# Columns of the norm gain in a PSUM bank of their own, and the second group's input issued by GpSimd: a start-up edit in a one-core convolution and MLP kernel

## The chip, the cores and the metric

The kernel runs on one core of a Trainium2 chip. The metric is the device time of one execution in microseconds (us). A profiled execution also has a span, from its first to its last instruction; times inside a profile are counted from the start of that span.

## What is computed

The reference has two blocks, one after the other. x is (8, 4224, 192) in float32, with 8 heads of 24 channels and 7 taps a head; the second block has a hidden width of 768. The weights of the second block arrive as float64.

```python
# block 1: lightweight convolution, causal, 7 taps per head
w = exp(weight - max(weight)); w = w / (sum(w) + 1e-9)       # (8 heads, 7 taps)
out[b, s, h, :] = sum_k w[h, k] * x_padded[b, s + k, h, :]    # 6 zero rows in front

# block 2: norm, two matrix products, residual
xn = (x - mean(x)) / sqrt(var(x) + 1e-6) * g_ln
result = x + relu(xn @ w_ch1) @ w_ch2
```

## The kernel before

**Groups.** The sequence positions lie on the 128 partitions. The work is cut into 18 groups of at most 16 positions a partition (`groups`, L70). Group 0 has 6 positions of batch 0. Group 1 has the 128 positions left over at the end of each of the 8 batches, 16 partitions a batch and 8 positions a partition. Group 2 has 10 positions, and all later ones 16. The loop at L963 takes one group at a time: up projection, the next group's convolution and transposition, down projection, result. It loads x of group g + 2 (L966), so x of groups 0 and 1 are loaded in the start-up.

**Start-up.** All instructions are issued in program order on each engine; there is no planner. What waits for what follows from the tiles that they share. The part that the edit touches is this:

- ScalarE's DMA queue loads the taps' raw weights (L197) and g in two pieces (L199, L200) into one row on one partition.
- TensorE spreads the raw weights over the 128 partitions by a product with a row of ones (L203), and turns g from a row into two columns, one a half (L205). Both write the same PSUM bank, `spread`.
- VectorE and ScalarE compute the softmax of the taps there (L268 to L277). ScalarE copies g's columns to `gs` (L273).
- SP's DMA queue loads w_ch1 (L211, L215), x of group 0 (`load_x(0)`: L164 twice, for partitions 16 to 127 and 1 to 15, and L171 for partition 0), x of group 1 (`load_x(1)`: L139 eight times, one DMA a batch of 16 partitions), and w_ch2 (L221), in this order.
- GpSimd writes the constants: averages (`share`, L296 and L297), a matrix `copy` (L299, L302), `less` (L306), `unit` (L312, L313), and the tap matrices of the last head (L319), which need the taps. ScalarE writes those of the two heads before (L327).
- float64 is turned into float32 by VectorE and ScalarE in `split_words` (L233 to L242) and `join_words` (L247 to L259). For w_ch1 `join_words` multiplies by g (L258), so it needs `gs`.

**After that, in TensorE's order.** `keep_warm(20)` (L939, L376) multiplies constants into a bank that nobody reads. `centre_w1` (L340) takes the mean out of w_ch1: L343, a convolution of one head of group 0 by matmuls (`conv_on_pe`, L334), L346, a second head, then three sets of four banks (L358, L363), with the third head behind the first set. ScalarE copies each bank of these sets to `w1` (L368). The first up projection (`up(0)`, L538) follows. The other five heads of group 0 are convolved by VectorE (L422), starting from a first tap on ScalarE (L397).

**PSUM.** There are 8 banks, handed out in a ring. `take_bank` gives the next one; `take_set` rounds up to the next bank whose number is a multiple of four and gives four:

```python
def take_set():
    i = (turn[0] + 3) // 4 * 4 % 8
    turn[0] = i + 4
    return all_banks[:, i : i + 4]
```

A matmul into a bank waits until the last reader of that bank is done. `up(0)` writes its set in the order q = 0 to 3, one bank a q.

Of the kernel before, what the change touches and what calls it, by code (L numbers as in the profile page):

```python
# [16 lines left out]
def kernel(  # L17
# [29 lines left out]
    nc = tc.nc  # L47
    PSUM = bass.MemoryType.PSUM
    B, S, D = x.shape
    H, K = weight.shape  # L50
    F = moe_w_ch1.shape[1]
    P = 128
# [66 lines left out]
    def take_bank():  # L119
        i = turn[0] % 8  # L120
        turn[0] = i + 1
        return all_banks[:, i]
# [9 lines left out]
    def load_x(g, queue=nc.sync):  # L132
        b, j0, n = groups[g]
        t = xpool.tile([P, J + PAD, D], F32, tag="xg", name=f"xg{g}")
        xg[g] = t
        flat = t.rearrange("p j d -> p (j d)")
        if b is None:
            for b in range(B):
                queue.dma_start(  # L139
                    out=flat[LP * b : LP * b + LP, 0 : (PAD + n) * D],  # L140
                    in_=bass.AP(
                        tensor=x.tensor, offset=(b * S + P * R - PAD) * D,
                        ap=[[n * D, LP], [1, (PAD + n) * D]],
                    ),
                )
            return
        if j0:
            queue.dma_start(
                out=flat[:, 0 : (n + PAD) * D], in_=xr[b, :, (j0 - PAD) * D : (j0 + n) * D]
            )  # L150
            return
        if b:

            queue.dma_start(
                out=flat[:, 0 : (PAD + n) * D],
                in_=bass.AP(
                    tensor=x.tensor, offset=(b * S - PAD) * D, ap=[[R * D, P], [1, (PAD + n) * D]]
                ),
            )
            nc.gpsimd.memset(t[0:1, 0:PAD, :], 0.0)  # L160
            return
        nc.gpsimd.memset(t[0:1, 0:PAD, :], 0.0)
        for p0, p1 in ((16, P), (1, 16)):
            nc.sync.dma_start(  # L164
                out=flat[p0:p1, 0 : (PAD + n) * D],
                in_=bass.AP(
                    tensor=x.tensor, offset=(b * S + p0 * R - PAD) * D,
                    ap=[[R * D, p1 - p0], [1, (PAD + n) * D]],
                ),
            )  # L170
        nc.sync.dma_start(out=flat[0:1, PAD * D : (PAD + n) * D], in_=xr[b, 0:1, 0 : n * D])  # L171
# [5 lines left out]
    gs = consts.tile([P, 2], F32, name="gs")  # L177
# [5 lines left out]
    def carve(n, dtype):  # L183
        part = room[:, taken[0] : taken[0] + n].bitcast(dtype)
        taken[0] += n
        return part
# [8 lines left out]
    row, ones = carve(H * K + 2 * P, F32)[0:1], carve(P, F32)[0:1]  # L195
    g_row = row[:, H * K :]
# [4 lines left out]
    nc.vector.memset(ones, 1.0)  # L201
    spread = take_bank()
    nc.tensor.matmul(spread[:, 0 : H * K], ones, row[:, 0 : H * K], start=True, stop=True)  # L203
    for r in range(2):
        nc.tensor.matmul(  # L205
            spread[:, H * K + r : H * K + r + 1], g_row[:, P * r : P * r + P], ones[:, 0:1],
            start=True, stop=True,
        )
    raw_taps = spread[:, 0 : H * K].rearrange("p (h k) -> p h k", k=K)

    nc.sync.dma_start(  # L211
# [5 lines left out]
            in_=w1_words[P:D, 2 * FH * r : 2 * FH * (r + 1)],  # L217
        )
    load_x(0)
    load_x(1)  # L220
    nc.sync.dma_start(  # L221
        out=raw2.rearrange("p (c d) w -> p c (d w)", d=D),
        in_=w2_words.rearrange("(c p) d -> p c d", p=P),
# [7 lines left out]
    def split_words(raw, mant, power):  # L231
        hi = raw[:, :, 1]
        nc.vector.tensor_single_scalar(mant.bitcast(U32), hi, 0xFFFFF, op=ALU.bitwise_and)  # L233
        nc.scalar.activation(mant.bitcast(F32), mant, AF.Relu, scale=2.0**-20, bias=1.0)
        nc.vector.tensor_scalar(
            out=power.bitcast(U32), in0=hi, scalar1=20, scalar2=0x7FF,
            op0=ALU.logical_shift_right, op1=ALU.bitwise_and,
        )
        nc.vector.tensor_scalar(
            out=power, in0=power, scalar1=896.0, scalar2=1151.0, op0=ALU.max, op1=ALU.min  # L240
        )
        nc.scalar.activation(power, power, AF.Relu, scale=float(1 << 23), bias=low)  # L242

    def join_words(dst, raw, mant, power, g=None):
        lo, hi = raw[:, :, 0], raw[:, :, 1]
        mant, power = mant.bitcast(F32), power.bitcast(U32)
        nc.vector.scalar_tensor_tensor(  # L247
            out=mant, in0=lo, scalar=2.0**-52, in1=mant, op0=ALU.mult, op1=ALU.add
        )
        nc.vector.scalar_tensor_tensor(  # L250
            out=power, in0=hi, scalar=0x80000000, in1=power,
            op0=ALU.bitwise_and, op1=ALU.bitwise_or,
        )
        power = power.bitcast(F32)
        if g is None:
            nc.vector.tensor_tensor(dst, mant, power, op=ALU.mult)
            return
        nc.vector.scalar_tensor_tensor(  # L258
            out=dst, in0=mant, scalar=g, in1=power, op0=ALU.mult, op1=ALU.mult  # L259
        )  # L260
# [9 lines left out]
        taps, raw_taps, wmax.unsqueeze(2).to_broadcast([P, H, K]), op=ALU.subtract  # L270
    )
    nc.scalar.activation(taps, taps, AF.Exp)
    nc.scalar.copy(gs, spread[:, H * K : H * K + 2])  # L273
    nc.vector.tensor_reduce(wsum, taps, axis=AX.X, op=ALU.add)
    nc.vector.tensor_scalar(wsum, wsum, scalar1=1e-9, scalar2=None, op0=ALU.add)
    nc.vector.reciprocal(wsum, wsum)
# [23 lines left out]
    for q in range(NQ):  # L300
# [19 lines left out]
        out=diag[:, H - 1 - PE_HEADS[0]], in_=taps[:, H - 1, :].unsqueeze(2).to_broadcast([P, K, P]),  # L320
        pattern=[[0, K], [-1, P]], compare_op=ALU.is_equal, fill=0.0, base=0, channel_multiplier=1,
    )

    def tap_matrices(ks):
        for k in ks:
            for i, h in enumerate(PE_HEADS[:-1]):
                nc.scalar.mul(diag[:, i, k, :], unit, taps[:, h, k : k + 1])  # L327
# [44 lines left out]
    def keep_warm(times):  # L372

        idle = take_bank()
        for _ in range(times):
            nc.tensor.matmul(idle[:, 0:P], less, copy, start=True, stop=True)  # L376

    tap_matrices(range(3))
    split_words(*words_a)
    tap_matrices(range(3, K))  # L380
    join_words(w1f[:, 0:2].rearrange("p s f -> p (s f)"), *words_a, ga)
    split_words(*words_b)
# [5 lines left out]
    def first_tap(g, heads=(0, H)):  # L388
        n = groups[g][2]
        if g == 1:  # L390

            y[g] = y[0][:, groups[0][2] :]
        elif heads[0] == 0:
            y[g] = ypool.tile([P, J, D], F32, tag="y", name=f"y{g}")
        for h in range(*heads):
            cs = slice(h * GRP, h * GRP + GRP)
            nc.scalar.mul(y[g][:, 0:n, cs], xg[g][:, 0:n, cs], taps[:, h, 0:1])  # L397
# [538 lines left out]
                add_and_store(g, js, D - C)  # L936


    keep_warm(20)  # L939
    first_tap(0, heads=(0, PE_HEADS[0]))  # L940

    early = CH * C // GRP
# [98 lines left out]
```

## Time and profile before

| what | value |
|---|---|
| median of 4 runs | 965.15 us (964.58 to 965.78) |
| profiled execution, its own time | 965.93 us |
| its span | 964.1 us |
| TensorE busy | 951.9 us, 99% of the span |
| VectorE busy | 897.9 us, 93% |
| ScalarE busy | 681.0 us, 71% |
| GpSimd busy | 250.3 us, 26% |
| SP's DMA queue (hardware_dynamic) | 6512 packets, 63.31 MB |
| GpSimd's DMA queue (software_dynamic) | 19120 packets, 99.36 MB |

Engines are called PE (TensorE's matmuls), PEld (its weight loads), DVE (VectorE), ACT (ScalarE), POOL (GpSimd) and SP. A q behind a name is the queue that issues for that engine. A float32 matmul has two passes, and each is an instruction of its own. Busy time is a sum over the whole span; what a step is worth is read from the stage in which it stands.

### The profile page before, as it was taken

To read this page: it belongs to the slowest core of one execution; us is meant where nothing else is said; L and a number is where in the kernel's file an instruction comes from. 1 tells how busy PE (TensorE), PEld (TensorE's weight loads), DVE (VectorE), ACT (ScalarE), POOL (GpSimd) and SP (SyncE) were. 2 spreads that over 40 slices of the span, in tenths; PEclk is the share of its full clock that TensorE was granted. 3 is DMA by queue.
4 is the path that set the end of the run, shared out by engine and by line. 5 is a ranking of instruction groups with operands and counts; after the bars stand their busy time and mean duration, and the time that the engine had idled before them with its cause. 6 is when DMAs were issued, how large, how long until landed. Compare 5 with 4: busy or idle time off the path is not lost.

```text
span 964.1 us, 38399 instructions
## 1 busy us (share of the span) xinstructions
PE 951.9 (99%) x17280; PEld 717.8 (74%) x17280; DVE 897.9 (93%) x1506; ACT 681.0 (71%) x1098; POOL 250.3 (26%) x383
## 2 busy tenths in 40 slices
PE   7999999999999999999999999999999999999997
PEld 6886586776858677686968778695867868586787
DVE  6999998989999999999999999999989999999867
ACT  5724669587787959687795968779696877867361
POOL 2004411612116131432116131341215221161300
PEclk9999999999999999999999999999999999999999
DMA  9343787769788796969788796978779697767031
GB/s 176 121 124 133 155 214 179 196 123 281 143 240 162 202 203 121 278 134 256 143 231 166 168 246 123 276 139 239 156 176 234 117 281 138 176 136 127 3 68 68
DMA packets 25802, 165.12 MB, mean 171 GB/s; under 512 B 3109, under 2 KB 4006, under 8 KB 17831
## 3 DMA queue, kind: packets, MB, share of 16 engines
q0 software_dynamic: 19120, 99.36, 53.5%
q1 hardware_dynamic: 6512, 63.31, 18.1%
q8 instruction: 135, 2.21, 0.9%
q14 instruction: 29, 0.24, 0.1%
q10 hardware_dynamic: 6, 0.00, 0.0%
HBM read 38.93 MB, written 50.33 MB: 93 GB/s over the span
## 4 chain that ended last, share of the span: by engine, by line
PE 94%; DMA 2%; DVE 2%; POOL 1%; issue 0%; ACT 0%; SPq 0%; DVEq 0%; POOLq 0%; ACTq 0%
PE ps L538 46%; PE ps L812 41%; PE ps L759 6%; DMA xg<-in_x_dram 1%; DVE room L779 1%; DMA room<-room 1%; PE ps L334 1%; DVE room L640 0%; ACT room L634 0%; PE ps L358 0%; PE ps L363 0%; POOL room L601 0%; POOL d L465 0%; DVE y L904 0%; POOL r L488 0%
## 5 line engine op out<-in xcount | busy, mean ns | idle before, releaser
L422 DVE SCALAR_TENSOR_TENSOR y<-xg,taps,y 128x384 f32<-128x384 f32 (+3 forms) x734 | 367.3, 577 | 0.2
L812 PE MATMUL ps<-room,w2sums 128*32 128x256 f32 (+1 forms) x4320 | 235.9, 375 | 0.2
L538 PE MATMUL ps<-yt,w 32*128 32x256 f32 (+2 forms) x4104 | 235.8, 379 | 0.1
L634 ACT COPY room<-ps 128x1024 f32<-128x1024 f32 (+1 forms) x132 | 172.0, 1303 | 79.1 <-PE ps L538 78.4
L538 PEld LDWEIGHTS ps<-yt,w 32*128 32x128 f32 x4104 | 204.8, 185 | 26.3 <-issue 9.6
L812 PEld LDWEIGHTS ps<-room,w2sums 128*32 128x32 f32 x4320 | 137.7, 110 | 93.2 <-ACT room L647 5.6
L812 PE MATMUL ps<-room,w 128*32 128x256 f32 (+1 forms) x3240 | 180.4, 375 | 0.1
L779 DVE TENSOR_TENSOR room<-room 128x1024 f32<-128x1024 f32 (+1 forms) x135 | 151.0, 1192 | 6.4 <-PE ps L812 6.4
L812 PEld LDWEIGHTS ps<-room,w 128*32 128x32 f32 x3240 | 104.0, 110 | 68.9 <-DVE room L640 5.2
L538 PE MATMUL ps<-ysums,w1sums 32*128 32x256 f32 x2160 | 125.1, 379 | 0.1
L538 PEld LDWEIGHTS ps<-ysums,w1sums 32*128 32x128 f32 x2160 | 108.8, 185 | 11.3 <-ACT room L634 3.6
L647 ACT ACTIVATE room<-room 128x1024 f32<-128x1024 f32 (+1 forms) x74 | 90.7, 1249 | 11.3 <-DMA room<-parts_cs 10.9
L818 ACT COPY cs<-ps 128x256 f32<-128x256 f32 (+1 forms) x180 | 66.6, 371 | 44.2 <-PE ps L812 44.2
L890 ACT ACTIVATE ot<-ot,r 128x192 f32<-128x192 f32 x232 | 93.8, 463 | 0.0
L897 POOL DMA_DIRECT2D out_dram<-ot x40 | 34.3, 1086 | 202.3 <-ACT ot L890 125.9
L397 ACT ACTIVATE y<-xg,taps 128x384 f32<-128x384 f32 (+3 forms) x141 | 72.7, 610 | 7.1 <-DMA out_dram<-y 6.9
L640 DVE TENSOR_TENSOR room<-room,ps 128x2048 f32<-128x2048 f32 (+1 forms) x20 | 42.5, 2127 | 35.9 <-PE ps L538 35.7
L453 DVE BATCH_NORM_STATS2 st<-y 128x6 f32<-128x192 f32 x264 | 70.2, 344 | 0.0
L538 PE MATMUL ps<-yt,w1sums 32*128 32x256 f32 x1080 | 65.3, 380 | 0.1
L818 ACT COPY room<-ps 128x256 f32<-128x256 f32 (+1 forms) x90 | 33.7, 374 | 43.8 <-PE ps L812 34.1
L538 PE MATMUL ps<-ysums,w 32*128 32x256 f32 x1080 | 64.5, 376 | 0.0
L408 ACT ACTIVATE tb<-xg,taps 128x384 f32<-128x384 f32 x112 | 62.0, 637 | 0.0
(109 smaller groups left out, 884.7 us busy)
## 6 DMA issues: line engine op xcount, KB each, us to landing
xg<-in_x_dram SPq DMA_DIRECT2D x15, 2112.0 KB, 17.7
out_dram<-ot POOLq DMA_DIRECT2D x29, 768.0 KB, 9.3
y<-tb POOLq DMA_DIRECT2D x28, 768.0 KB, 10.5
room<-room POOLq DMA_DIRECT2D x42, 512.0 KB, 5.3
out_dram<-y SPq DMA_DIRECT2D x13, 1536.0 KB, 9.6
room<-parts_cs POOLq DMA_DIRECT2D x14, 1024.0 KB, 8.2
room<-parts_tb POOLq DMA_DIRECT2D x14, 1024.0 KB, 7.6
xg<-in_x_dram SPq DMA_DIRECT2D x1, 1536.0 KB
```

Of the source, the lines that this page charges most:

```text
L397: nc.scalar.mul(y[g][:, 0:n, cs], xg[g][:, 0:n, cs], taps[:, h, 0:1])
L408: nc.scalar.mul(tb[g][:, 0:n, cs], xg[g][:, 1 : 1 + n, cs], taps[:, h, 1:2])
L422: nc.vector.scalar_tensor_tensor(out=y[g][:, 0:n, cs], in0=t[:, k : k + n, cs], scalar=taps[:, h, k : k + 1], in1=y[g][:, 0:n, cs], op0=AL ...
L453: nc.vector.bn_stats(out=sums[g][:, j, :], in_=y[g][:, j, :])
L538: nc.tensor.matmul(banks[:, q, i * w : i * w + w], right[rows, c, P * i : P * i + P], left[rows, :, c, :], start=(first and c == 0 and i = ...
L634: nc.scalar.activation(dst, src, AF.Relu) if relu else nc.scalar.copy(dst, src)
L647: nc.scalar.activation(c, c, AF.Relu)
L759: nc.tensor.matmul(bank[C * q : C * q + C, 0:w], w2[:, f, C * c : C * c + C], left, start=(f == 0), stop=(f == NF - 1),)
L779: nc.vector.tensor_tensor(a[:, *dst, f], a[:, *left, f], a[:, *right, f], op=op)
L812: nc.tensor.matmul(dst[C * q : C * q + C, 0:w], right[:, f, C * c : C * c + C], left[:, f, q], start=(first and f == PAIR), stop=(f == PAI ...
L818: nc.scalar.copy(to[:, c], dst[:, 0:w].rearrange("p (j t) -> p j t", t=t))
L890: nc.scalar.mul(ots[g][:, j, :], ots[g][:, j, :], rstd[g][:, j : j + 1])
```

## The change

Three things are edited, all in the start-up. g's columns are taken out of `spread` and get a bank of their own, `g_cols`; the 20 idle matmuls that stood in front of the first tap now stand before `tap_matrices`, 12 ahead of the two column matmuls and 8 behind them, with a bank each. The copy to `gs` moves behind the first `split_words` on ScalarE. `load_x(1)` is taken from SP's queue, where it stood between x of group 0 and w_ch2, and is issued by GpSimd behind L319, the last of its constants.

```diff
@@ -201,11 +201,6 @@
     nc.tensor.matmul(spread[:, 0 : H * K], ones, row[:, 0 : H * K], start=True, stop=True)
-    for r in range(2):
-        nc.tensor.matmul(
-            spread[:, H * K + r : H * K + r + 1], g_row[:, P * r : P * r + P], ones[:, 0:1],
-            start=True, stop=True,
-        )
     raw_taps = spread[:, 0 : H * K].rearrange("p (h k) -> p h k", k=K)
@@ -217,7 +212,6 @@
     load_x(0)
-    load_x(1)
     nc.sync.dma_start(
@@ -270,7 +264,6 @@
     nc.scalar.activation(taps, taps, AF.Exp)
-    nc.scalar.copy(gs, spread[:, H * K : H * K + 2])
     nc.vector.tensor_reduce(wsum, taps, axis=AX.X, op=ALU.add)
@@ -321,6 +314,8 @@
+    load_x(1, nc.gpsimd)
+
     def tap_matrices(ks):
@@ -375,8 +370,16 @@
             nc.tensor.matmul(idle[:, 0:P], less, copy, start=True, stop=True)
+    keep_warm(12)
+    g_cols = take_bank()
+    for r in range(2):
+        nc.tensor.matmul(
+            g_cols[:, r : r + 1], g_row[:, P * r : P * r + P], ones[:, 0:1], start=True, stop=True
+        )
+    keep_warm(8)
     tap_matrices(range(3))
     split_words(*words_a)
+    nc.scalar.copy(gs, g_cols[:, 0:2])
     tap_matrices(range(3, K))
@@ -936,7 +939,6 @@
-    keep_warm(20)
     first_tap(0, heads=(0, PE_HEADS[0]))
```

## The prediction, made before the run

> **What bounds the kernel now.** I read the page's chain of work first. TensorE carries 94% of it, DMA 2%.
>
> ```profile
> span 964.1 us, 38399 instructions
> ...
> PE 94%; DMA 2%; DVE 2%; POOL 1%; issue 0%; ACT 0%; SPq 0%; DVEq 0%; POOLq 0%; ACTq 0%
> ```
>
> So the end is set by when TensorE starts real work and by the holes after that. The edit touches only the first 30 us. Next view: the chain in order of time there (start, length, what).
>
> ```profile
> 2.48 0.58 SPq L164
> 3.06 0.05 issue
> 3.11 13.84 DMA xg<-in_x_dram
> 16.95 0.14 issue
> 17.08 1.95 PE ps L334 x14
> ...
> 27.60 0.65 PE ps L363 x8
> 28.25 13.15 PE ps L538 x288
> ```
>
> Nothing but the arrival of x of group 0 (16.95) decides when L334 starts. From 17.08 on TensorE is back to back. The third view, the timeline, has the work before the arrival and the first hole after it (start, length, engine, line; in brackets the idle time before).
>
> ```profile
> 4.62 0.21 POOL L306 MEMSET room<- 128x128 f32 x1
> ...
> 5.05 0.29 POOL L313 TENSOR_SCALAR_AFFINE_SELECT room<-room 128x128 f32<-128x128 f32 x1
> ...
> 7.84 7.38 PE L376 MATMUL ps<-room 128*128 128x128 f32 x40
> 7.94 0.22 DVE L268 TENSOR_REDUCE wmax<-ps 128x8 f32<-128x56 f32 x1 [6.88 <-PE ps L205]
> ...
> 9.70 1.24 POOL L319 TENSOR_SCALAR_AFFINE_SELECT room<-taps 128x896 f32<-128x896 f32 x1 [4.35 <-DVE taps L277]
> ...
> 15.30 1.56 PE L343 MATMUL ps<-room 128*128 128x384 f32 x4
> ...
> 26.97 3.16 ACT L368 COPY w<-ps 128x384 f32<-128x384 f32 x8 [1.20 <-PE ps L363]
> ```
>
> The softmax of the taps (L268 to L277) waits for g's columns; GpSimd (L319) and ScalarE (L327) wait for the taps. All of it is done before x lands. Fourth view, the DMA issues (count, KB each, us to landing):
>
> ```profile
> xg<-in_x_dram SPq DMA_DIRECT2D x8, 168.0 KB, 10.7
> raw<-in_moe_w_ch_dram SPq DMA_DIRECT2D x1, 1152.0 KB, 9.9
> xg<-in_x_dram SPq DMA_DIRECT2D x1, 1008.0 KB, 13.0
> ...
> xg<-in_x_dram SPq DMA_DIRECT2D x1, 135.0 KB, 13.8
> ```
>
> x of group 0 is 1008 + 135 + 4.5 KB. Behind it, in the same SP queue, stand the eight 168 KB pieces of group 1's x, then w2. I linked the trace's packet records into engines by end and next start. Each engine writes its w1 rows, then 7 or 8 rows of 9216 B of group 0, then one 10752 B row of each piece of group 1. Most engines start group 0's rows between 5.5 and 7.6 us and are done between 10.6 and 12.7. One starts at 8.42, ends its last row at 15.27, and its completion is the 16.95. A row takes about 0.57 us until 10.7, when the first group-1 rows begin; then 1.4 to 1.7.
>
> [...] from 163.5 to 169 us, engines holding both GpSimd's queue (1536 B, 0.14 us) and SP's (12288 B, 0.47 us) mostly alternate one for one. [...] group 1's pieces, each on 16 partitions, take 1.05 to 1.15 us a row on all engines, 16 x 10752 B / 1.1 us = 156 GB/s with two pieces overlapping, against some 255 GB/s for group 0's rows. [...] L235 took 1.34 us beside L319, 0.36 us for half the size later. [...] The trace shows only the warming: L376 matmuls start 0.213 us apart until 13.41 and 0.111 us after, 5.57 us from 7.84.
>
> **Part 1, g's columns apart.** L268 can follow L203 (ends 2.78), so at about 2.85 instead of 7.94. From L268 to L319 it is 9.70 - 7.94 = 1.76 us: taps at 4.6. GpSimd is busy until 5.34, so L319 runs 5.4 to 6.6. w1 lands at 7.15 (semaphore records), so L233 moves from 9.55 to about 7.2. Idle matmuls start at 4.87 (behind L306); 24 passes at 0.213 plus a slow first end near 10.2, the two columns near 11. The copy of gs, now behind split_words on ScalarE, then waits until about 11.2 (split_words ends by 9.7); queued behind it is half of tap_matrices (8 x 0.305 = 2.4 us, ends 13.7), and L258 waits for gs too. It ends near 12.4 instead of 15.24. The second idle batch runs out at 13.0 (warm) to 14.6 (cold). L343 ends near 14.6 instead of 16.86. What hides all this is the wait for x: worth 0 unless x lands before 16.95, and then at most 17.08 - 14.9 = 2.2 us.
>
> **Part 2, one bank more.** Two more take_bank calls per start (g's own, a second idle batch) shift the ring by two. Counting calls: before, the last eight L368 copies free banks 3,4,5,6 then 7,0,1,2, and the first set of up(0) is 4 to 7; its fourth matmul waits for the fifth copy (28.46 + 0.52 = 28.98; that matmul starts at 29.04). After, they free 5,6,7,0 then 1,2,3,4, and the set is 0 to 3; its fourth matmul waits for the seventh copy (29.20 + 0.55 = 29.75). In order, all of up(0) stands behind it: **+0.77 us** on the path. Later sets shift by four throughout and cost 0.
>
> **Part 3, x of group 1 on GpSimd.** SP's own issues get shorter: w2 follows group 0's x at once and lands early, wanted only at 28.66. Gain 0. Group 1's x is wanted at 32.85 (L397), so its own lateness costs 0. GpSimd has no other work until 77 us. But the eight issues, queued behind L319, now start at 6.6. Issues at 103 to 107 us come 0.5 us apart; the one at 96.94 has its first packet at 98.58, 1.64 us later. So group-1 rows enter the engines at about **8.3 us instead of 10.7**, in their own queue, and alternate with group 0's rows instead of following them. The late engine at that moment still has all 8 rows of group 0. Its floor without group 1: 8.42 + 8 x 0.5 + 1.7 to completion = 14.1. With strict alternation it writes 8 x 0.57 + 7 x 1.12 = 12.4 us: 20.8, landing 22.5. By bytes: some 664 KB of group 0 at 260 and 7/8 of 1376 KB at 156 GB/s are 2.55 + 7.7 = 10.3 us: 18.7, landing 20.4. [...] If rows of group 1 cost it only 0.66 (half the engines at them), 8.6 us: landing 18.7. I take 20.2: **+3.3 us**; bounds -2.2 and +5.5.
>
> **Sum.** +3.3 + 0.77 = +4.1 us on the profiled execution: 965.93 (span 964.1 and 1.8 around it) gives 970.0. The four runs' median is 0.8 lower, 965.15: **969.2 us**.
>
> **Rivals.** (1) *The clock falls too.* TensorE is idle from about 14.6 to 20.2, 5.6 us. [...] the matmuls after the arrival start at half speed; at 5.57 us until warm, as at the start, that loses 2.4 more: 971.6. [...] Against: no restart in the trace, [...] and a later L343 shortens the gap. (2) *x is not delayed*: [...] the late engine is spared; landing within 1 us of 16.95, bank shift alone: 965.9. For it: the same bytes move. Against: the alternation at 164 us. (3) *Not slower, faster*: [...] (1.4 to 1.7 us a row became 0.57 again) and lands at 14.5; part 1 then pays 2.2 - 0.77 = 1.4: 963.7. It decides if group-1 rows enter after about 12 us; my reading of the issue times has them at 8.3. This would also be the case in which spreading the idle matmuls does what it says.
>
> **Numbers.** Forecast, x late with a warm clock: 0.45, own range 967.1 to 970.6. (1) 0.26, to 973.5. (2) 0.20, 964.7 to 967.1. (3) 0.09, 962.5 to 964.7. A change within 0.2% (1.93 us: 963.2 to 967.1) can't be told from none. Slower is the forecast and (1), 0.70 with an edge of (2) off and on; same is (2) and most of (3), 0.25; faster the deep end of (3), 0.05. The range 965.0 to 972.6 leaves out (3) and the ends, under 0.2.
>
> **What would show it.** In the profile after: L268 near 2.9 and L319 near 5.4; GpSimd's queue with 10752 B packets from 8 to 9 us; the chain's DMA piece ending near 20 instead of 16.95; L343 ending near 14.6; the first full row of L538 about 1.6 us behind the last L363 instead of 0.8; the interval of L334 matmuls 0.122 us (warm) or double. I am wrong if group-1 packets start after 11 us or if x lands before 17.

## The result, and the profile after

The changed kernel takes **967.77 us** (median of 44 runs, 965.07 to 971.04); the kernel before takes 965.34 us beside it (62 runs, 964.02 to 969.02). The ratio is 1.0023, 95% interval 1.0019 to 1.0028: slower by 2.4 us, just above the 0.2% that can be told from no change. The profiled execution took 967.13 us, with a span of 965.3, 1.2 over that of before. The forecast number was 969.2, and it was off by 1.4 us. Its mechanism was wrong: x of group 0 landed earlier (12.51, from the semaphore records, instead of 16.95), not later, and the loss arose some 15 us further on.

The page's span and chain of work. DMA's share has doubled, from 2% to 4%:

```profile
span 965.3 us, 38415 instructions
...
PE 93%; DMA 4%; DVE 1%; POOL 1%; ACT 0%; issue 0%; ACTq 0%; POOLq 0%; DVEq 0%
```

The chain in order of time (start, length, what) shows which DMA it is. Before, x of group 0 held it until 16.95; now it is w2 (`raw`), until 28.73, and then the split of w2 on VectorE and ScalarE, up to an eviction (L531):

```profile
0.80 4.95 DMA room<-in_moe_w_ch_dram
...
5.76 22.97 DMA raw<-in_moe_w_ch_dram
...
28.76 0.76 DVE spare L227
29.52 0.68 DVE spare L229
...
32.18 0.80 ACT room L531
...
33.02 9.76 PE ps L541 x192
42.79 11.84 PE ps L762 x288
```

The timeline of TensorE has the front of it (start, length; in brackets the idle time before). The first products of `centre_w1` (L338, L343 before) follow at once on the idle matmuls (L371; the 24 instructions of its line are `keep_warm(12)`, two a matmul), and the first convolution (L329, L334 before) on L338: it starts at 13.84 instead of 17.08 and waits for no DMA. Then `up(0)` breaks after 96 instructions:

```profile
4.88 5.33 PE L371 MATMUL ps<-room 128*128 128x128 f32 x24 [2.04 <-POOL room L299]
...
12.55 1.46 PE L338 MATMUL ps<-room 128*128 128x384 f32 x4
13.84 1.88 PE L329 MATMUL ps<-xg,room 128*128 128x144 f32 x14
...
25.38 5.31 PE L541 MATMUL ps<-yt,w 32*128 32x192 f32 x96 [0.41 <-ACT w L363]
33.02 9.76 PE L541 MATMUL ps<-yt,w 32*128 32x192 f32 x192 [2.34 <-ACT room L531]
```

In the kernel before, `up(0)` ran without such a break, and VectorE started w2's split without waiting for the DMA:

```profile
28.07 13.33 PE L538 MATMUL ps<-yt,w 32*128 32x192 f32 x288
...
28.66 0.72 DVE L233 TENSOR_SCALAR spare<-raw 128x1152 uint32<-128x1152 uint32 x1
```

In the changed kernel two engines stood ahead of the break, each waiting: VectorE for w2, and ScalarE for VectorE. The eviction (ScalarE's copy of a finished bank out of PSUM) that TensorE needs stands behind them in ScalarE's order:

```profile
28.76 0.76 DVE L227 TENSOR_SCALAR spare<-raw 128x1152 uint32<-128x1152 uint32 x1 [2.66 <-DMA raw<-in_moe_w_ch_dram]
...
29.55 1.16 ACT L228 ACTIVATE spare<-spare 128x1152 f32<-128x1152 int32 x1 [2.70 <-DVE spare L227]
...
31.02 1.26 ACT L236 ACTIVATE spare<-spare,low 128x1152 int32<-128x1152 int32 x1 [0.30 <-DVE spare L233]
32.18 0.79 ACT L531 ACTIVATE room<-ps 128x768 f32<-128x768 f32 x1
```

The DMA issues (count, KB each, us from issue to landing): w2 took 9.9 us before and takes 23.0 now; group 0's 1008 KB took 13.0 and take 9.3.

```profile
xg<-in_x_dram POOLq DMA_DIRECT2D x8, 168.0 KB, 12.6
raw<-in_moe_w_ch_dram SPq DMA_DIRECT2D x1, 1152.0 KB, 23.0
...
xg<-in_x_dram SPq DMA_DIRECT2D x1, 1008.0 KB, 9.3
```

After the break the granted clock is halved for one stretch. In the table of stretches, the columns are length, busy time of PE, PEld, DVE, ACT and POOL with counts, PEclk, DMA share, GB/s:

```profile
26.97:30.38 3.41, 3.41 (x87) 3.41 (x82) 1.59 (x3) 0.83 (x1) 0.00 (x0) 1.00 1.05 374
30.38:33.79 3.41, 1.07 (x21) 0.78 (x23) 3.32 (x4) 3.11 (x6) 0.00 (x0) 1.00 0.61 245
33.79:37.20 3.41, 3.41 (x49) 3.41 (x48) 3.41 (x8) 3.24 (x8) 0.00 (x0) 0.50 0.00 0
37.20:40.62 3.42, 3.42 (x88) 3.42 (x88) 3.42 (x12) 1.02 (x2) 0.00 (x0) 1.00 0.02 5
```

So the account up to the start of `down(0)` (41.33 before, 42.72 after) is, from the starts in the two timelines: first convolution -3.24; from there to the first full row of `up(0)` (its seventh instruction, at 26.53 and 29.04) 12.69 instead of 11.96, **+0.73**; from there to its third set of banks (instruction 97, at 33.02 and 33.08) 6.49 instead of 4.04, **+2.45**; from there to `down(0)` 9.70 instead of 8.25, **+1.45**, which is the halved clock (with a break but no halving it is 8.27, in the run with ten idle fills below). Together +1.39, of which the span keeps 1.2.

### The profile page after: what moved, and what is told of

Its sections match the earlier page's. It is cut to its first block, busy times and chain, and to the rows that moved or that the text cites. A ratio compares the mean times of both kernels' runs of the same rounds, so it can differ in the third digit from the quotient of the medians.

```text
span 965.3 us, 38415 instructions
## 1 busy us (share of the span) xinstructions
PE 952.6 (99%) x17280; PEld 718.8 (74%) x17280; DVE 897.7 (93%) x1506; ACT 680.9 (71%) x1098; POOL 251.7 (26%) x391
## 4 chain that ended last, share of the span: by engine, by line
PE 93%; DMA 4%; DVE 1%; POOL 1%; ACT 0%; issue 0%; ACTq 0%; POOLq 0%; DVEq 0%
PE ps L541 46%; PE ps L815 42%; PE ps L762 6%; DMA raw<-in_moe_w_ch_dram 2%; DMA room<-room 1%; DMA room<-in_moe_w_ch_dram 1%; DVE room L643 0%; DVE room L782 0%; ACT room L637 0%; POOL room L604 0%; POOL d L468 0%; DVE y L907 0%; POOL r L491 0%; POOL d L487 0%; POOL d L486 0%
```

## The theory after the result, and its rivals

**Theory.** GpSimd's rows enter the engines after group 0's, not among them, so x of group 0 is early: it lands at 12.49 to 13.95 in the ten profiles in which group 1's rows come behind it in another queue or behind w2, against 16.95 and 14.82 in the two in which they follow it directly in SP's queue. But they then share each engine with w2, which the change left alone in SP's queue. The packet records don't name their engine; linked by end and next start, one such chain from 15.4 us on reads (`a` is a 10752 B row of group 1, `B` a 1536 B row of w2, us each):

```
a1.22 B0.23 a1.17 B0.21 B0.26 B0.25 B0.26 B0.23 a1.21
```

In the stretch from 13 to 25 us, taken in steps of 2 us, GpSimd's rows have 10.6 to 12.7 of the 16 engines and w2's 3.5 to 5.9 (26 to 42 GB/s). At 25.0 us 497 of w2's 768 rows are through. Group 1's last row ends at 25.26, and at 27.0 w2 has 758. VectorE was free for w2 at 28.76 - 2.66 = 26.10.

**Rivals.** (a) The bank shift is the loss. (b) Taking x of group 1 out of SP's queue is the loss, in whichever queue it goes. (c) GpSimd's first packets are late because VectorE splits w1 beside their issue (L227, L229 and L233, 5.77 to 7.74), and an issue behind that brings them sooner.

## Experiments

All kernels compute the whole of the reference. Each ratio is against the kernel before, run beside it.

### Group 1's x back on SP, behind w2

```diff
         in_=w2_words.rearrange("(c p) d -> p c d", p=P),
     )
+    load_x(1)
...
-    load_x(1, nc.gpsimd)
```

> The changed kernel with group 1's x put back on SP's queue, but behind w2 instead of ahead of it. Theory A (the edit's front gains 3.2 us because group 1's rows no longer follow group 0's in one queue; the loss is w2, whose rows share the engines with group 1's and land at 28.7, so that the split of w2 holds ScalarE, the evictions of up(0) and TensorE for 2.3 us and its clock halves for 3.4 us): x of group 0 lands near 12.5, the first L334 matmul near 13.8, w2 lands before 20, no hole inside up(0), total near 965.3 - 3.2 + 0.8 = 962.9. Theory B (the early landing is an accident of one profile and the bank shift is what the edit costs): x of group 0 lands near 17 in some profile, total 966. Theory C (the recorded forecast: group 0's x is late because of GpSimd's queue): better than the changed kernel, but not better than the kernel before by more than 0.2 us.

Measured: 963.34 us (962.52 to 964.71, 12 runs) against 965.58; 0.9979 (0.9971 to 0.9988). The rest of the change stands, yet it is 4.4 us faster than with GpSimd's issue. The issues of this kernel, and its `up(0)` in TensorE's timeline:

```profile
xg<-in_x_dram SPq DMA_DIRECT2D x8, 168.0 KB, 11.0
raw<-in_moe_w_ch_dram SPq DMA_DIRECT2D x1, 1152.0 KB, 12.8
```

```profile
25.66 13.21 PE L540 MATMUL ps<-yt,w 32*128 32x192 f32 x288 [0.41 <-ACT w L362]
```

w2 lands 12.8 us after its issue, its split starts at 26.31, and the 288 instructions of `up(0)` run in one piece. The first convolution starts at 14.13, about where the changed kernel had it. With w2 ahead of group 1 the loss is gone. Since group 1 is back in SP's queue here, this run alone doesn't decide rival (b). It falls with two runs below that have group 1 in GpSimd's queue and don't lose: GpSimd's issue alone, and sixteen idle fills.

### The same with two spare banks

```diff
     keep_warm(8)
+    take_bank(), take_bank()
     tap_matrices(range(3))
```

(on top of the kernel just shown)

> As e1_x1_behind_w2, with two more bank calls whose banks nobody uses, so that the ring stands four further than in the kernel before instead of two. Bank theory: the hole between the last L363 matmul and the first full row of the up projection is 0.8 us instead of 1.57, and the time is 0.77 us below e1_x1_behind_w2, near 962.1. Rival: ScalarE's copies are behind anyway and the difference is under 0.3 us.

Measured: 963.36 us (961.69 to 965.67, 16 runs); 0.9978 (0.9971 to 0.9986), no different from the run without them. The two calls undo the shift of the ring, and the first full row does start 25.61 - 24.82 = 0.79 behind the end of the last L357 instead of 26.81 - 25.25 = 1.56, and `up(0)` starts without the 0.41 of idle time. But TensorE then stops a little later:

```profile
24.64 5.13 PE L541 MATMUL ps<-yt,w 32*128 32x192 f32 x96
30.10 8.56 PE L541 MATMUL ps<-yt,w 32*128 32x192 f32 x192 [0.33 <-ACT room L531]
```

### g's columns alone, and GpSimd's issue alone

The first is the changed kernel with `load_x(1)` back between group 0 and w2 on SP; the second is the kernel before with only group 1's x moved.

```diff
     load_x(0)
+    load_x(1)
...
-    load_x(1, nc.gpsimd)
```

> Only the part with g's columns, the idle matmuls and gs; group 1's x stands on SP between group 0's x and w2, as before. Theory A: the taps are ready at 4.7 but x of group 0 lands at 15 to 17 as before, w2 lands near 26 in its own queue, no stall of the split: the front gains 0 to 1, the bank shift costs 0.77, total 965.3 to 966.1. Theory B: the same as the changed kernel within 0.5 us, near 967.5, or as good as e1.

```diff
     load_x(0)
-    load_x(1)
...
+    load_x(1, nc.gpsimd)
+
     def tap_matrices(ks):
```

> Only the move of group 1's x to GpSimd behind L319, in the kernel before. L319 waits for the taps until 9.7, so the eight issues begin near 10.9. Theory A: x of group 0 lands near 12.5 but TensorE is held by L343 until 16.85, so the front gains 0.2 us; w2 shares the engines with group 1's x and lands near 29 to 30, wanted at 28.5: 0.5 to 1.5 us of stall, total 965.5 to 967. Theory C: group 1's rows come in too late to delay group 0's x, total 965.

Measured: 965.30 us (13 runs), 1.0001 (0.9992 to 1.0009), and 965.76 us (13 runs), 1.0004 (0.9995 to 1.0012). Neither half alone moves the time. With g's columns alone x of group 0 landed at 14.82, not at 16.95 as in the profile of before with the same queue: in the profile of before it came 1.68 us behind the last row (15.27), and why it is earlier here isn't shown. TensorE's timeline of that kernel shows both waits:

```profile
14.96 1.95 PE L328 MATMUL ps<-xg,room 128*128 128x144 f32 x14 [1.90 <-DMA xg<-in_x_dram]
...
32.42 3.82 PE L540 MATMUL ps<-yt,w 32*128 32x192 f32 x84 [0.58 <-ACT room L530]
```

With GpSimd's issue alone the issues start at 10.27, behind the late taps, and the first packets at 14.82; x of group 0 is through at 12.12. The first convolution then starts at 16.06, held by L344, which ends at 16.2: the idle matmuls on TensorE, and the softmax and the first join of w1 on VectorE, have to be done before it, and all still stand behind g's columns. The gain of the queue needs the gain of the columns to be seen, and in the kernel that has both w2 is late.

### w2's split later

```diff
+            if g == 0 and f == 2:
+                split_words(*words_2)
+                join_words(w2flat, *words_2)
             if 1 <= f <= 4:
...
-    split_words(*words_2)
-    join_words(w2flat, *words_2)
     store_y(0)
```

> The changed kernel with the split and join of w2 moved from ahead of up(0) to behind its third eviction; the transfers stay as in the changed kernel. Theory A (w2's lateness costs only because ScalarE's part of the split stands ahead of the evictions): w2 still lands near 28.7, the hole of 2.3 us inside up(0) is gone, the clock isn't halved after it, 0.3 us may be lost at the end of up(0): 963.3 to 964, about as e1_x1_behind_w2. Theory B (the loss is in the bank shift or in transfers beside later work): within 0.7 us of the changed kernel's 967.8.

Measured: 971.99 us (970.69 to 973.01, 5 runs); 1.0071 (1.0059 to 1.0084). I had expected the gain of the first experiment; it became the second slowest run. The break in `up(0)` is indeed gone, and a larger one stands ahead of `up(1)`:

```profile
25.20 13.54 PE L541 MATMUL ps<-yt,w 32*128 32x192 f32 x288 [0.41 <-ACT w L363]
38.77 11.91 PE L765 MATMUL ps<-room,w 128*32 128x192 f32 x288
56.43 3.85 PE L541 MATMUL ps<-yt,w 32*128 32x256 f32 x36 [5.75 <-DVE yt L436]
```

VectorE's timeline says why:

```profile
37.31 1.36 DVE L250 TENSOR_TENSOR w<-spare 128x1152 f32<-128x1152 f32 x1
38.59 15.88 DVE L425 SCALAR_TENSOR_TENSOR y<-xg,taps,y 128x192 f32<-128x192 f32 x48
54.50 1.78 DVE L436 STREAM_TRANSPOSE yt<-y 128x1536 f32<-128x1536 f32 x1
```

The join of w2 (L250) waits for ScalarE's late part of the split and stands ahead of group 1's whole convolution on VectorE (15.88 us), which starts at 38.59 instead of 34.98 in the changed kernel. There the transposition behind it (L436) was done at 52.67, ahead of `up(1)` at 54.55; here it ends at 56.28. From 52.95, inside the idle time before `up(1)`, to 59.78 the clock was halved as well. The run shows that w2's split is the wait inside `up(0)`, and that moving it back only hands the wait on.

### Group 1's x earlier, and later, on GpSimd

First, ahead of GpSimd's constants:

```diff
     copy, less, mean = carve(P, F32), carve(P, F32), carve(F, F32)
+    load_x(1, nc.gpsimd)
...
-    load_x(1, nc.gpsimd)
```

> The changed kernel with group 1's x issued by GpSimd ahead of its constants, near 1.9 us. The recorded mechanism (rows of two queues alternate in each engine, so group 0's x is late): first packets of GpSimd's queue near 3.4 to 4, group 0's last packet at 17 to 21 instead of 11.5, total 968 to 972. Rival (GpSimd's rows enter only when the SP queue's big rows are through, whatever the issue time): first packets near 12 again, group 0's x as in the changed kernel, total 967 to 969 with the constants 4 us later.

Measured: 973.99 us (971.75 to 975.22, 4 runs); 1.0090 (1.0075 to 1.0104). Issued from 1.80 on, its packets start at 4.67, before group 0's (8.14), and they do alternate with them: group 0's 1008 KB take 17.4 us from issue to landing, 9.3 in the changed kernel. The issues, and the front of TensorE's timeline:

```profile
xg<-in_x_dram POOLq DMA_DIRECT2D x8, 168.0 KB, 14.3
raw<-in_moe_w_ch_dram SPq DMA_DIRECT2D x1, 1152.0 KB, 19.1
...
xg<-in_x_dram SPq DMA_DIRECT2D x1, 1008.0 KB, 17.4
```

```profile
17.09 1.46 PE L337 MATMUL ps<-room 128*128 128x384 f32 x4
21.56 3.34 PE L328 MATMUL ps<-xg,room 128*128 128x144 f32 x14 [3.01 <-DMA xg<-in_x_dram]
```

GpSimd's constants come later too, so the idle matmuls start only at 9.68, but the chain of waits holds only x. x of group 0 lands at 21.43, and the first 14 matmuls, 1.88 us in the changed kernel, take 3.34 with a mean granted clock of 0.59 (21.5 to 25.0). This is the forecast's mechanism together with its first rival, in the kernel that lets rows of group 1 in early.

Then behind ten and behind sixteen idle fills, which move the issue to 9.63 and to 11.21 (6.22 in the changed kernel):

```diff
+    idler = carve(P, F32)
+    for _ in range(10):
+        nc.gpsimd.memset(idler, 0.0)
     load_x(1, nc.gpsimd)
```

> The changed kernel with ten memsets of an unused tile on GpSimd ahead of the issues of group 1's x, which then begin near 8 instead of 6.2. [...] If GpSimd's rows enter when group 0's are through: near 12.3 as before, time as the changed kernel. If the lag is fixed at 6.1 us: near 14, w2 lands earlier than 28.7, time 966 to 967.

> The changed kernel with sixteen memsets of an unused tile on GpSimd ahead of the issues of group 1's x, which then begin near 11.8 instead of 6.2 (9.6 with ten memsets). If what costs is that rows of group 1 share the engines with w2's: most of w2 is through before they enter, w2 lands before 24, no hole inside up(0), 963.3 as e1_x1_behind_w2; unless group 1's x then lands after 29.3, where its first tap wants it, and gives part back. If GpSimd's queue itself costs something: over 964.2.

Measured: with ten 964.25 us (962.80 to 965.52, 12 runs), 0.9990 (0.9982 to 0.9999); with sixteen 964.39 us (962.54 to 966.35, 21 runs), 0.9988 (0.9981 to 0.9994). First packets came at 14.90 and 14.56. In the profile of the first, w2 still landed at 27.99 and TensorE still waited; in that of the second w2 was there 11.6 us after its issue, and `up(0)` ran in one piece:

```profile
32.27 8.33 PE L544 MATMUL ps<-yt,w 32*128 32x192 f32 x192 [1.30 <-ACT room L534]
```

```profile
raw<-in_moe_w_ch_dram SPq DMA_DIRECT2D x1, 1152.0 KB, 11.6
```

```profile
25.42 13.71 PE L544 MATMUL ps<-yt,w 32*128 32x192 f32 x288 [0.41 <-ACT w L366]
```

What counts is how much of w2 has gone ahead when group 1 enters. At 15.0 us 291 of w2's 768 rows were through in the changed kernel, 681 with ten idle fills and 746 with sixteen. In these profiles the last rows, which then have to share, decide when the whole has landed. The two medians are alike although w2 was late in one of the two profiles; how often it is late in either kernel isn't shown. The second is also above the 964.2 that I had named as the sign that GpSimd's queue itself costs something. Its interval overlaps that of the first experiment, so a small cost of that queue is neither shown nor excluded.

Rival (c) has no support: with ten idle fills the issue stood 3.4 us later, behind those three steps (6.46 to 8.23 in this profile), and the packets came only 2.6 us later, still 5.27 us behind it.

### The changed kernel with two spare banks

```diff
     keep_warm(8)
+    take_bank(), take_bank()
     tap_matrices(range(3))
```

> The changed kernel with two more bank calls whose banks nobody uses. If the bank shift is part of what the edit costs: the first full row of up(0) comes 0.77 us earlier against the last L363 matmul, and the time falls by about 0.8 us, to 967.0. If the late w2 sets when the third pair of banks is free whatever the first rows did: the row comes earlier, the hole inside up(0) grows by the same 0.77 us, and the time stays within 0.3 us of 967.8; a longer hole may even halve the clock more often and make it slower.

Measured: 968.61 us (967.13 to 972.50, 9 runs); 1.0032 (1.0019 to 1.0046). Undoing the shift doesn't bring 0.77 us back. The first full row starts earlier (26.02 for 26.53), and TensorE's break grows from 2.34 to 3.66:

```profile
33.84 9.66 PE L542 MATMUL ps<-yt,w 32*128 32x192 f32 x192 [3.66 <-ACT room L532]
```

w2's split started at 29.58 in this profile, 0.82 later than in the changed kernel's, and the third set starts at 33.84, also 0.82 later. Rival (a) falls.

### g's columns further forward

On top of the first experiment: 7 idle matmuls ahead of g's columns and 13 behind them, then 10 ahead and 8 behind.

```diff
-    keep_warm(12)
+    keep_warm(7)
     g_cols = take_bank()
...
-    keep_warm(8)
+    keep_warm(13)
```

> e1_x1_behind_w2 with 7 idle matmuls ahead of g's columns and 13 behind, instead of 12 and 8. gs is written near 8.9 instead of 11.1, so the first join and L343's matmuls come 1.1 us earlier, and the first convolution matmul waits for x of group 0 (13.1 to 13.6) instead of for them (14.1). Theory A: 0.5 to 1 us below e1_x1_behind_w2, near 962.6. Rival: x of group 0 lands too late in most runs for it to matter, 963.3.

```diff
-    keep_warm(12)
+    keep_warm(10)
     g_cols = take_bank()
```

> e1_x1_behind_w2 with 10 idle matmuls ahead of g's columns instead of 12, still 8 behind. The first join, and L343's matmuls with it, come up to 0.8 us earlier; x of group 0 lands near 13.1 to 13.6, so the first convolution matmul can start 0.4 us earlier. 0.3 to 0.5 us below e1_x1_behind_w2, 962.9; if the clock warms later instead, as with 7 ahead and 13 behind, 963.5 or more.

Measured: 964.29 us (962.24 to 965.91, 13 runs), 0.9993 (0.9984 to 1.0001), a miss; and **962.98 us** (961.49 to 965.80, 16 runs), 0.9973 (0.9965 to 0.9980), better than both kernels; it has the lowest median of all, though its interval overlaps that of the first experiment. In the first the clock rose only at 12.89 (9.90 in the changed kernel, where the idle matmuls' starts go from 0.213 to 0.111 us apart), so the 26 idle passes behind the columns ran at the halved clock up to then, and the convolution waited for L337:

```profile
9.10 4.96 PE L370 MATMUL ps<-room 128*128 128x128 f32 x26
13.90 1.46 PE L337 MATMUL ps<-room 128*128 128x384 f32 x4
15.19 1.88 PE L328 MATMUL ps<-xg,room 128*128 128x144 f32 x14
```

## Why the number was right and the reasons were not

One relation runs through the profiles. All times are from the timelines, in us; "third set" is the start of instruction 97 of `up(0)`, the first into its third set of banks, which needs the first set's eviction.

| kernel | first convolution | w2's split starts | third set | difference | `down(0)` |
|---|---|---|---|---|---|
| before | 17.08 | 28.66 | 33.08 | 4.42 | 41.33 |
| changed | 13.84 | 28.76 (for w2) | 33.02 | 4.26 | 42.72 |
| changed, two spare banks | 14.06 | 29.58 (for w2) | 33.84 | 4.26 | 43.44 |
| g's columns alone | 14.96 | 28.16 (for w2) | 32.42 | 4.26 | 40.69 |
| ten idle fills | 14.09 | 28.01 (for w2) | 32.27 | 4.26 | 40.54 |
| GpSimd's issue alone | 16.06 | 28.03 | 32.25 | 4.22 | 40.52 |
| sixteen idle fills | 13.88 | 26.07 | 30.30 | 4.23 | 39.06 |
| behind w2 | 14.13 | 26.31 | 30.54 | 4.23 | 38.80 |
| behind w2, two spare banks | 13.69 | 25.88 | 30.10 | 4.22 | 38.59 |
| behind w2, 10 idle ahead | 13.71 | 24.86 | 30.12 | 5.26 | 38.32 |

In these kernels the third set starts no earlier than 4.22 us after VectorE's first step of w2's split. The three left out are the two in which the first full row itself came later (6.64 with GpSimd's issue first, 6.99 with 7 idle matmuls ahead) and the one whose split was moved behind these matmuls (1.06). "(for w2)" marks the kernels in which that step waited for the DMA; in the others VectorE came to it later than w2. The last column isn't the whole time: what follows it took 923.98 to 926.87 us in these profiled executions. So differences of a microsecond or two are judged by the medians, and the profiles say where they arise.

**Part 1** was right in its times: the softmax starts at 2.88 (2.85 forecast), L312 runs from 5.29 (5.4), the gs copy is at 10.77 (11.2), and L338 ends at 14.0 (14.6). The first split of w1 came earlier than forecast, at 5.77 (7.2). Its ceiling of 2.2 us for an early x was too low because the convolution starts with L338's end, here 13.84.

**Part 2** was right in its place and wrong in its worth. The first full row of `up(0)` started 1.56 us behind the last L358 (24.97), as forecast: the seventh L363 copy, which frees its bank, ended at 26.47, and the row started at 26.53. But "in order, all of up(0) stands behind it" left out that the third set waits for an eviction behind w2's split. With the shift undone the row was earlier, and the wait behind it as much longer: 963.36 for 963.34, and 968.61 for 967.77. The 0.73 of the account would only move into the 2.45; the term is 0 in these kernels, not 0.77.

**Part 3** failed in two steps. "Group-1 rows enter the engines at about 8.3 us": the issues did start at 6.22 (6.6 forecast), but the first packet came at 12.33, 6.1 us after its issue instead of 1.64 (a lag read at 97 us, where nothing of SP's was in flight). Group 0's last packet had ended at 11.54. So the third rival's front came true ("if group-1 rows enter after about 12 us"), and +3.3 became -3.24. The floor of 14.1 for x was too high as well: it kept the late engine of one profile, while in the profile after every row of group 0 ended by 11.54. Two of this part's sums don't come out with its own row times: at 0.57 us a row the floor is 14.7, and 8 x 0.57 + 7 x 0.66 is 9.2, not 8.6. Neither changes the 20.2 that was taken. "w2 ... lands early, wanted only at 28.66. Gain 0": w2 landed at 28.73. Both halves were mistaken. It didn't land early, because the alternation that I had worked out for group 0 struck w2 instead, and there one row of 1.2 us stood against one to five of 0.23. And 28.66 was the need of the kernel before; with the convolution 3.2 us earlier VectorE wanted it at 26.10. That wait, +2.45, paid back most of the gain.

**The first rival's clock** came in another place. It was to fall in the gap ahead of x; it fell behind the break in `up(0)` and cost 1.45 in this profile. The stretch of 3.41 us ahead of the halved one had TensorE busy for 1.07 (see the end). In the profile of before the clock is halved too, once, from 962.31, behind a stretch of 3.41 us with TensorE busy for 0.07; so "the trace shows only the warming" was wrong. When the rival's drop would come was the author's estimate. Over the 44 runs, the 14 with a mean granted clock of 0.999 or more average 966.6 us and the 30 below 968.3. That the lower ones are those with such a stretch is argued from one profile, not shown for each.

The near hit of the number is thus a coincidence of sums: +3.3 and +0.77 forecast, against -3.24, +0.73, +2.45 and +1.45. The profiles give 1.2 and the medians 2.4; the profiled executions stand 0.6 above the median of before and 0.6 below that of after. So about half of the 2.4 is accounted for by one pair of profiles.

**Open.** What holds GpSimd's first packets back while SP's queue is busy isn't settled (the lag goes with SP's packets in flight, but isn't proportional to them), nor which DMA engine lags with x of group 0, and why.

## What to carry to other kernels

When a transfer is moved to another queue, work out the landing of what stood behind it as well as of what stood ahead of it: here two queues shared the engines row by row, one row of 1.2 us against one to five of 0.23, and the transfer with the small rows took 23.0 us instead of 9.9. A need time read from the profile before moves forward with what is gained ahead of it (here from 28.66 to 26.10, with the convolution 3.24 earlier), so cover must be priced again at the new time. Ahead of a late load, look down the order of the engine that waits: here evictions stood behind it, and TensorE behind them.

## What was not expected of the hardware

- **GpSimd's first packet comes late while SP's packets run.** In the profile of the changed kernel, most later issues from GpSimd find none of SP's packets running up to their own first one, and the lag is 1.42 to 1.53 us. Where SP's packets ran it was 4.26 us (issued at 115.92, 95 of them in between), 3.51 (171.32, 98) and, in the start-up, 6.11 (6.22, 387). The start-up of the other kernels had 2.87 us (issued at 1.80), 6.43 (6.22, w2's split later), 6.28 (6.22, two spare banks), 5.27 (9.63), 4.55 (10.27) and 3.35 (11.21). That SP's packets are the cause is not shown.
- **The clock was halved after a stretch that was not all idle.** The stretch from 30.38 to 33.79 had TensorE busy for 1.07 of 3.41 us, and the next one, to 37.20, was at 0.50; the break was 2.34 us. In all 13 profiles the time between two changes of the clock is a whole multiple of 3.41 us, so it can be cut into stretches of this length. Of those at full speed, all 17 with TensorE busy for up to 1.36 us (the highest from 958.80 in the changed kernel) were followed by half speed, and none of the 3607 with 1.41 us or more (the lowest from 956.07 in the first experiment). Others are 0.98 (from 17.57, GpSimd's issue first) and 1.14 (from 49.54, w2's split later), both halved, and 2.11 (from 28.86, ten idle fills), not halved. So in these profiles the edge lies between 1.36 and 1.41 us of 3.41, near 40%, by the profile's busy time, in which the ends of matmuls are modelled. What sets it is not shown.
- **One load landed at two times with the same queue order.** x of group 0 landed at 16.95 in the profile of before and at 14.82 with g's columns alone. In the first, 123 of its 127 rows of 9216 B had ended by 12.73, and the last four at 13.31, 14.22, 14.29 and 15.27; in the changed kernel all had by 11.54, and it landed at 12.51.
